# A linear-attention and gated-MLP block on one core: another order of work between the first stage and the z2 stage

## The chip, the cores and the metric

The kernel runs on one core of a Trainium2 chip. The metric is the device time of one execution in microseconds (us). Three executions of the kernel before took 614.0, 615.39 and 615.52 us, with a median of 615.39. Beside them there is one profiled execution, from which all rows of the profile come.

The engines are named as in the profile: PE (TensorE, matmuls; PEld its weight loads), DVE (VectorE), ACT (ScalarE), POOL (GpSimd) and SP (SyncE, which here only issues transfers). Each engine works through its own instructions in a fixed order. A name with a q behind it (SPq, ACTq, POOLq) is the issue of a transfer by that engine.

## The reference

The input x has 2048 rows of 512. It is normalised, and two branches are added to it.

```python
def _A_ref(x, wqkv, w_phi, wo):          # 32 heads of 16
    q, k, v = split(x @ wqkv)
    pq, pk = q @ w_phi, k @ w_phi        # per head
    phi_q = concat(softmax(pq), softmax(-pq))
    phi_k = concat(softmax(pk), softmax(-pk))
    kv, z = phi_k^T v, sum_s phi_k
    return (phi_q kv) / (phi_q z + 1e-6) @ wo

def _B_ref(x, w_in, w_sp, b_sp, w_out):  # F = 1376, halves of 688
    z = gelu(x @ w_in)
    z1, z2 = z[..., :688], layernorm(z[..., 688:])
    g = w_sp @ z2 + b_sp                 # over the rows
    return (z1 * g) @ w_out

xn = layernorm(x)
return x + _A_ref(xn, ...) + _B_ref(xn, ...)
```

All is in float32.

## The kernel before

The rows are worked on in NT = 16 tiles of 128. A float32 operand is held as two parts: `h`, the rounded value (`round_h`, line 61 on ACT), and `l`, the remainder (`rest_l`, line 65, a subtraction, on DVE unless another engine is given). A product is three matmuls, `ah*bh`, `ah*bl` and `al*bh` (`mm3`, lines 69 to 71), so these three lines carry nearly all matmuls.

**First stage** (lines 201 to 501). For each tile: projections for v and for k and q (the small matrix w_phi is first folded into the weights for k and q), and for both of these the two softmaxes (`softmax_pair`, line 120). That takes the maximum and minimum per head (lines 123, 124), two subtractions that write the shifted values (132, 133, "shift"), one exp on ACT (135), sums per head (137) and a reciprocal (138). For k, `normalise` (340) multiplies by the reciprocals on DVE, and a transfer issued by POOL adds the tile to `zacc` (341). `add_kv` (348) adds the tile to the bank `kvps` in matmuls of 32 by 64, with e as one operand and v as the other. For q, the tile of exps is stored to `e_d` (336) for later. Tiles of x are transposed on PE for tiles 0 to 4; for the others a transposed copy of x is loaded (`raw`, 297) and the row means are added to it by a transfer (`nm_d`, 307 and 311). `fetch_T(s)` issues the load of `raw` for a tile and then that of the next plain tile `xt` (208), which has three buffers and is needed for the row statistics (281).

The B branch's input product is split: the first 512 columns of z1 are computed per tile by `z1_raw` (163) with the weight `w1`. This takes 12 matmuls into one of two banks of the PSUM pool `za`, a drain by ACT into the tile `z1f` (168), and a store issued by ACT (169). Of the 16 tiles the loop of the first stage does 11; LAG = 5 are left to the next part.

The weight for everything else, `w2`, has two halves of 432 columns. The raw first half, `w2_raw` (the profile's `w_raw`), has memory of its own and is loaded by eight transfers on SP's queue (`fetch_w2(0, ...)`, lines 174 and 175; written at tile 8 of the loop). The second half is loaded into `staged` tiles (`w2s`) over memory of the first stage.

**The part between** (lines 596 to 668). It splits the two halves of w2 (`split_w2`, `made0` and `made1`), does the last z1 tiles, masks kv (`masked_kv`, 618, into `kvm`, read from `kvps`), sums zacc over the rows on PE (`make_zb`, tile `pz`, and a copy `zb`, 613), transposes kv (`make_kvT`: four transposes 628, a copy on ACT 630, an add on DVE 631), prepares the first operands A of the later stage (`prep_a`: sums S on DVE, 587 to 591, and splits of `wf`, 61 and 65), and weighs two tiles of q's features (`early_features`, 534 to 550, and a transpose 643).

**The z2 stage** (lines 726 to 759). `z2_proj` computes a tile's product with both halves of w2 in 24 matmuls (`zps`). The four pairs of banks are used in turn: the pool of kv, `zc` (which takes the banks of `pz` and `kvt` over), `zb`, `za`. ACT applies gelu, DVE takes statistics, POOL computes the factor (104, 105, 751), and the tiles are normalised and made into operands B.

**Later stages.** The spatial product (`g`, a Strassen-like form with seven products), the gate, the attention output and the last projections.

The order of the instructions on each engine is set by a planner. It goes through the program with a timing model of its own, in which what stands earlier in the program has priority, and what is not ready lets later work pass. `with tc.issue_after(i):` binds what the block issues on the engine of instruction `i` to come behind `i` on that engine; instructions of other engines in the block are not bound. A tile in memory that another pool has used before waits for the tiles that it is laid over.

Of the kernel before, what the change touches and what calls it, by code (L numbers as in the profile page):

```python
# [53 lines left out]
def mixer(ctx: ExitStack, tc: tile.TileContext, x, x_t, wv, wqkT, phi_bd, wo, w_in, wst, b_r, w_out, out):  # L54
# [64 lines left out]

    def softmax_pair(pl, src, tag, scale=1.0, ebufs=2, blocks=1, behind=None):  # L120

        mm = pl.tile([P, 2, H], F32, tag=tag + "mm", bufs=1, name="mm")
        dve.tensor_reduce(mm[:, 0], heads(src), axis=AX.X, op=ALU.max)
        dve.tensor_reduce(mm[:, 1], heads(src), axis=AX.X, op=ALU.min)
        er = pl.tile([P, NF + 2 * H], F32, tag=tag + "e", bufs=ebufs, name="e")
        eb = er.rearrange("p (j c) -> p j c", j=blocks)
        e, r = eb[:, :, :NF // blocks], eb[:, :, NF // blocks:]
        e2 = e.rearrange("p j (h a d) -> p j h a d", a=2, d=DH)
        hd = src.rearrange("p (h j d) -> p j h d", j=blocks, d=DH)
        m = [mm[:, k].rearrange("p (h j) -> p j h", j=blocks).unsqueeze(3).to_broadcast([P, blocks, H // blocks, DH])  # L130
             for k in range(2)]
        dve.tensor_tensor(e2[:, :, :, 0], hd, m[0], op=ALU.subtract)
        softmax_pair.shifted = dve.tensor_tensor(e2[:, :, :, 1], m[1], hd, op=ALU.subtract).ins  # L133
        with tc.issue_after(behind) if behind else ExitStack():
            softmax_pair.exp = act.activation(e, e, AF.Exp, scale=scale).ins  # L135
        sm = pl.tile([P, 2 * H], F32, tag=tag + "sm", bufs=1, name="sm").rearrange("p (j h) -> p j h", j=blocks)
        dve.tensor_reduce(sm, e.rearrange("p j (h d) -> p j h d", d=DH), axis=AX.X, op=ALU.add)  # L137
        dve.reciprocal(r, sm)
        return er
# [12 lines left out]
    def z2_proj(ps, s, w, order):  # L152
# [6 lines left out]
        for k, j in enumerate(order):  # L159
            accumulated(p[k][:, :FW], s, *w[j])  # L160
        return [(slice(k, k + 1), p[k][:, :FW].unsqueeze(1)) for k in range(2)] if ps in (za, kv_ps_p) else [(slice(0, 2), q[:, :, :FW])]
# [15 lines left out]

    def split_w2(dst, raw):
        return [(round_h(act, dst[0][:, c], raw[c]), rest_l(dst[1][:, c], raw[c], dst[0][:, c])) for c in range(ND)]

    LAG = 5
    xT, ahead_of_run = [], []
# [18 lines left out]
    with ExitStack() as p0:  # L201
# [92 lines left out]
        def fetch_T(s):  # L294
            if s < NT:
                raws[s] = wk.tile([P, ND * P], F32, tag="raw", name="raw")
                sp.dma_start(raws[s], x_t[s].rearrange("p a b -> p (a b)"))
                fetch(s + 1)
# [35 lines left out]
        def proj_q(s):  # L334
            e = softmax_pair(wk, proj(s, wqk_h[:, 0], wqk_l[:, 0]), "q", r_x[:, s:s + 1], blocks=NB)
            pool.dma_start(e_d[s], e)

        def normalise(er):
            e = er[:, :NF]
            dve.tensor_tensor(heads(e), heads(e), bc(er[:, NF:], 2 * H), op=ALU.mult)  # L340
            normalise.last = pool.dma_start(zacc, e, accum_op=ALU.add).ins  # L341
# [114 lines left out]
        for s in range(NT):  # L456
# [35 lines left out]
            if s == NT // 2:  # L492
                fetch_w2(0, [w2_raw[:, c] for c in range(ND)])
            if s and s % 2 == 0:
                last = run([t for t in (s + 2,) if t < XT0], feats[:-1])
                behind.close()
                behind.enter_context(tc.issue_after(last))
                del feats[:-1]
        for t, e in feats:
            add_kv(t, e)  # L500
        behind.close()
# [96 lines left out]
    with ExitStack() as p1:  # L598
# [26 lines left out]
        def make_kvT(kvm):  # L625
            pt = psk.tile([P, NG, P], F32, tag="kvt", name="kvt")
            for g in range(NG):
                pe.transpose(pt[:, g], kvm[:, g], ident)
            pt = pt.rearrange("p g (a k b) -> p (g a) k b", k=2, b=QP)
            act.activation(kvT, pt[:, :, 0], AF.Copy)  # L630
            dve.tensor_tensor(kvT, kvT, pt[:, :, 1], op=ALU.add)  # L631

        with ExitStack() as p1a:
# [13 lines left out]
            early = [load_q(s, tb.tile([P, QW], F32, tag="et", bufs=2, name="et")) for s in range(NE)]  # L647
            made0 = split_w2(w2[0], [w2_raw[:, c] for c in range(ND)])[-1]
            for s in range(NT - LAG, NT):
                with tc.issue_after(made0[0]) if s > NT - LAG else ExitStack():  # L650
                    z1_raw(tmp1, s, 2)
                if s == NT - LAG + 1:
                    with tc.issue_after(made0[1]):
                        kvm = masked_kv()
                    with tc.issue_after(z1_raw.last), tc.issue_after(masked_kv.last):
                        made1 = split_w2(w2[1], raw2)[-1]
                if s == NT - 2:
                    make_zb(made1[1])
            with tc.issue_after(z1_raw.pe):
                make_kvT(kvm)  # L660
            raw[0], raw[1] = load_a(0), load_a(1)
            A[0] = prep_a(0, raw.pop(0))
            with tc.issue_after(made1[1]):
                for s in range(NE):
                    early_features(s)
# [61 lines left out]
    for s in range(NT):  # L727
        order = (0, 1) if s % 2 == 0 else (1, 0)
        with tc.issue_after(z1_raw.pe):
            p = z2_proj((kv_ps_p, zc, zbp, za)[s % 4], s, w2, order)  # L730
# [421 lines left out]
```

## Time and profile before

| | us |
|---|---|
| median of three executions | 615.39 |
| profiled execution: time | 615.62 |
| profiled execution: span of the profile | 613.9 |
| first stage: last projection of q issued on PE | 186.94 |
| first matmul of the z2 stage | 205.50 |
| first matmul of the spatial product g | 282.52 |

The span is what the profile covers, from the first to the last instruction or transfer; the 1.7 us beyond it lie around the execution. The granted clock of PE is at 1.00 in the stretches looked at. In the rows of a timeline the first number is the start in us from the span's start, the second the busy time; a bracket gives the idle time of the engine before the instruction and what ended it. Several alike are merged ("x4"). What ended an idle time is inferred from semaphores.

### The profile page before, as it was taken

How to read it: one execution, taken by the hardware profiler on the slowest of the kernel's cores; microseconds unless marked ns; L12 is line 12 of the kernel's file. 1: busy time of each engine (PE TensorE's matmuls, PEld its weight loads, DVE VectorE, ACT ScalarE, POOL GpSimd, SP SyncE). 2: the span in 40 equal slices, each digit the busy share in tenths (PEclk: the TensorE clock that was granted, in tenths of full speed). 3: DMA queues.
4: the chain of work that ended last, by engine and by line, in shares of the span. 5: the costliest groups of instructions: out<-in, count | busy, mean ns of one | idle time of the engine just before them, and what ended most of it. 6: DMA issues, size and time to landing. Idle time of an engine off the chain costs nothing.

```text
span 613.9 us, 11029 instructions
## 1 busy us (share of the span) xinstructions
PE 604.3 (98%) x4059; PEld 537.7 (88%) x4059; DVE 512.7 (84%) x902; ACT 305.3 (50%) x450; POOL 133.2 (22%) x241
## 2 busy tenths in 40 slices
PE   8999999999998999999999999999999999999997
PEld 6778888888887799999999999999999987777786
DVE  5798999999899998678987786878768588999973
ACT  4533333332434457677554545545455755567520
POOL 4243322223111034343000101011010312122200
PEclk9999999999999999999999999999999999999999
DMA  8639776665659720001438767576868989799931
GB/s 322 200 93 199 207 191 151 172 187 126 188 146 242 250 86 22 16 24 48 151 101 214 213 184 232 149 212 190 220 196 219 265 236 251 203 206 244 230 104 69
DMA packets 78322, 106.80 MB, mean 174 GB/s; under 512 B 36956, under 2 KB 46940, under 8 KB 78268
## 3 DMA queue, kind: packets, MB, share of 16 engines
q1 hardware_dynamic: 64268, 61.39, 36.8%
q0 software_dynamic: 11408, 39.98, 24.8%
q10 hardware_dynamic: 2592, 4.72, 2.1%
q8 instruction: 32, 0.52, 0.4%
q14 instruction: 22, 0.18, 0.1%
HBM read 60.30 MB, written 31.09 MB: 149 GB/s over the span
## 4 chain that ended last, share of the span: by engine, by line
PE 89%; DMA 5%; DVE 3%; issue 0%; ACT 0%; SPq 0%; DVEq 0%; ACTq 0%
PE g L70 11%; PE g L71 11%; PE g L69 11%; PE proj L69 6%; PE proj L70 6%; PE proj L71 6%; PE pout L69 6%; PE pout L71 5%; PE pout L70 5%; PE zps L69 4%; PE zps L70 4%; PE zps L71 4%; PE z1ps L69 2%; PE z1ps L70 2%; PE z1ps L71 2%; DMA xt<-in_x 2%
## 5 line engine op out<-in xcount | busy, mean ns | idle before, releaser
L70 PE MATMUL g<-B,A 128*128 128x344 f32 x448 | 143.1, 320 | 0.0
L71 PE MATMUL g<-B,A 128*128 128x344 f32 x448 | 143.1, 319 | 0.0
L69 PE MATMUL g<-B,A 128*128 128x344 f32 x448 | 143.0, 319 | 0.0
L69 PEld LDWEIGHTS g<-B,A 128*128 128x128 f32 x448 | 84.3, 188 | 0.0
L71 PEld LDWEIGHTS g<-B,A 128*128 128x128 f32 x448 | 84.2, 188 | 0.0
L70 PEld LDWEIGHTS g<-B,A 128*128 128x128 f32 x448 | 84.1, 188 | 0.0
L135 ACT ACTIVATE e<-e,r_x 128x1024 f32<-128x1024 f32 x32 | 36.7, 1149 | 62.7 <-DVE e L133 62.7
L61 ACT ACTIVATE A<-S 128x512 fp32r<-128x512 f32 x64 | 39.7, 628 | 52.1 <-PE g L71 24.1
L65 DVE TENSOR_TENSOR A<-S,A 128x512 fp32r<-128x512 f32 x64 | 43.6, 688 | 23.3 <-ACT A L61 22.6
L69 PE MATMUL proj<-wqk_h,xT 128*128 128x512 f32 x124 | 49.2, 396 | 0.0
L61 ACT ACTIVATE A<-wf 128x512 fp32r<-128x512 f32 x64 | 33.2, 521 | 32.1 <-PE g L71 26.3
L71 PE MATMUL proj<-wqk_h,xT 128*128 128x512 f32 x124 | 48.4, 390 | 0.0
L70 PE MATMUL proj<-wqk_l,xT 128*128 128x512 f32 x124 | 48.3, 390 | 0.0
L69 PE MATMUL zps<-w,xT 128*128 128x432 f32 x128 | 46.0, 360 | 1.2 <-DVE kvT L631 1.2
L65 DVE TENSOR_TENSOR A<-wf,A 128x512 fp32r<-128x512 f32 x64 | 35.4, 554 | 13.0 <-ACT A L61 12.6
L70 PE MATMUL zps<-w,xT 128*128 128x432 f32 x128 | 46.1, 360 | 0.0
L71 PE MATMUL zps<-w,xT 128*128 128x432 f32 x128 | 45.8, 358 | 0.0
L137 DVE TENSOR_REDUCE sm<-e 128x64 f32<-128x1024 f32 x32 | 38.5, 1205 | 2.0 <-ACT e L135 1.7
L341 POOL DMA_DIRECT2D zacc<-e x16 | 14.7, 918 | 76.3 <-DVE e L340 22.5
L61 ACT ACTIVATE oT<-po 128x512 fp32r<-128x512 f32 x16 | 8.7, 596 | 41.0 <-PE po L992 41.0
L69 PE MATMUL pout<-wu,uh 128*128 128x512 f32 (+1 forms) x75 | 29.0, 387 | 0.0
L69 PE MATMUL z1ps<-w,xT 128*128 128x512 f32 x64 | 25.4, 396 | 3.0 <-ACT z1f L168 1.6
(182 smaller groups left out, 1427.6 us busy)
## 6 DMA issues: line engine op xcount, KB each, us to landing
wf<-in_wst SPq DMA_DIRECT2D x64, 256.0 KB, 3.8
e_d<-e POOLq DMA_DIRECT2D x16, 544.0 KB, 5.1
et<-e_d SPq DMA_DIRECT2D x64, 136.0 KB, 5.2
zacc<-e POOLq DMA_DIRECT2D x16, 512.0 KB, 4.9
z1t<-z_d POOLq DMA_DIRECT2D x16, 344.0 KB, 6.2
u_d<-c POOLq DMA_DIRECT2D x14, 384.0 KB, 2.8
uT_d<-uT POOLq DMA_DIRECT2D x12, 384.0 KB, 3.2
ut<-uT_d SPq DMA_DIRECT2D x11, 384.0 KB, 7.5
```

The lines of the kernel that those rows point to most:

```text
L61: return act.activation(h, src, AF.Copy).ins
L65: return (eng or dve).tensor_tensor(l, src, h.bitcast(F32), op=ALU.subtract).ins
L69: pe.matmul(dst, ah, bh, start=start, stop=False)
L70: pe.matmul(dst, ah, bl, start=False, stop=False)
L71: return pe.matmul(dst, al, bh, start=False, stop=stop).ins
L135: softmax_pair.exp = act.activation(e, e, AF.Exp, scale=scale).ins
L137: dve.tensor_reduce(sm, e.rearrange("p j (h d) -> p j h d", d=DH), axis=AX.X, op=ALU.add)
L341: normalise.last = pool.dma_start(zacc, e, accum_op=ALU.add).ins
```

## The change

The change moves work around the end of the first stage, in six places:

- The load of w2's first half is bound behind the last transposed x tile that has been issued at that point of the loop (`fetch_T.last`, tile 12), on SP.
- z1 of tiles 11 and 12 is issued on PE behind the last q projection; the exp of that q tile on ACT is bound behind the drain of tile 12, and its two shifts on DVE behind the multiply of the last k tile. z1 of tile 13 follows, with its drain behind that exp. LAST = 2 tiles (14 and 15) are left for the part between, where `z1f` now has three buffers.
- kv of tiles 14 and 15 is bound on PE behind z1 of tile 13, so that both run together.
- In the part between: the roundings of w2's first half come behind the last exp, the masking of kv behind the last remainder of it, z1 of 14 and 15 behind the kv run on PE and their drains behind the roundings on ACT.
- The remainders of w2's second half go from DVE to POOL, behind POOL's issue of the last sum into zacc.
- On ACT, A's roundings come behind the copy of kvT; on DVE, the early features behind the add of kvT; on PE, z2's tiles come one after the other, the first behind the transposes of kv.

```diff
@@ softmax_pair(..., behind=None, shift_behind=None) @@
-        dve.tensor_tensor(e2[:, :, :, 0], hd, m[0], op=ALU.subtract)
-        softmax_pair.shifted = dve.tensor_tensor(e2[:, :, :, 1], m[1], hd, op=ALU.subtract).ins
+        with tc.issue_after(shift_behind) if shift_behind else ExitStack():
+            dve.tensor_tensor(e2[:, :, :, 0], hd, m[0], op=ALU.subtract)
+            softmax_pair.shifted = dve.tensor_tensor(e2[:, :, :, 1], m[1], hd, op=ALU.subtract).ins
@@
-    def split_w2(dst, raw):
-        return [(round_h(act, dst[0][:, c], raw[c]), rest_l(dst[1][:, c], raw[c], dst[0][:, c])) for c in range(ND)]
-
-    LAG = 5
+    def split_w2(dst, raw, eng=None):
+        return [(round_h(act, dst[0][:, c], raw[c]), rest_l(dst[1][:, c], raw[c], dst[0][:, c], eng)) for c in range(ND)]
+
+    LAG, LAST = 5, 2
@@ proj_q @@
-            e = softmax_pair(wk, proj(s, wqk_h[:, 0], wqk_l[:, 0]), "q", r_x[:, s:s + 1], blocks=NB)
+            p, behind = proj(s, wqk_h[:, 0], wqk_l[:, 0]), None
+            if s == NT - 1:
+                for n in range(2):
+                    with tc.issue_after(proj.last):
+                        z1_raw(wk, NT - LAG + n, 2)
+                behind = z1_raw.last
+            e = softmax_pair(wk, p, "q", r_x[:, s:s + 1], blocks=NB, behind=behind,
+                             shift_behind=normalise.dve if behind else None)
@@ the loop over tiles @@
             if s == NT // 2:
-                fetch_w2(0, [w2_raw[:, c] for c in range(ND)])
+                with tc.issue_after(fetch_T.last):
+                    fetch_w2(0, [w2_raw[:, c] for c in range(ND)])
@@ behind the loop @@
+        for n in range(NT - LAG + 2, NT - LAST):
+            with tc.issue_after(softmax_pair.exp):
+                z1_raw(wk, n, 2)
         for t, e in feats:
-            add_kv(t, e)
+            with tc.issue_after(z1_raw.pe):
+                last = add_kv(t, e)
@@ the part between @@
-            made0 = split_w2(w2[0], [w2_raw[:, c] for c in range(ND)])[-1]
-            for s in range(NT - LAG, NT):
-                with tc.issue_after(made0[0]) if s > NT - LAG else ExitStack():
-                    z1_raw(tmp1, s, 2)
-                if s == NT - LAG + 1:
-                    with tc.issue_after(made0[1]):
-                        kvm = masked_kv()
-                    with tc.issue_after(z1_raw.last), tc.issue_after(masked_kv.last):
-                        made1 = split_w2(w2[1], raw2)[-1]
-                if s == NT - 2:
-                    make_zb(made1[1])
+            with tc.issue_after(softmax_pair.exp):
+                made0 = split_w2(w2[0], [w2_raw[:, c] for c in range(ND)])[-1]
+            with tc.issue_after(made0[1]):
+                kvm = masked_kv()
+            for s in range(NT - LAST, NT):
+                with tc.issue_after(made0[0]), tc.issue_after(last):
+                    z1_raw(tmp1, s, 3)
+                if s == NT - LAST:
+                    with tc.issue_after(normalise.last):
+                        made1 = split_w2(w2[1], raw2, pool)[-1]
+                    make_zb(masked_kv.last)
             with tc.issue_after(z1_raw.pe):
                 make_kvT(kvm)
             raw[0], raw[1] = load_a(0), load_a(1)
-            A[0] = prep_a(0, raw.pop(0))
-            with tc.issue_after(made1[1]):
+            with tc.issue_after(make_kvT.act):
+                A[0] = prep_a(0, raw.pop(0))
+            with tc.issue_after(make_kvT.dve):
                 for s in range(NE):
                     early_features(s)
@@ the z2 stage @@
-        with tc.issue_after(z1_raw.pe):
+        with tc.issue_after(z2_proj.pe if s else make_kvT.pe):
             p = z2_proj((kv_ps_p, zc, zbp, za)[s % 4], s, w2, order)
```

The rest of the diff keeps the instructions that are named here (`fetch_T.last`, `normalise.dve`, `z2_proj.pe`, `make_kvT.pe`, `.act`, `.dve`).

More of the change, by code (lines that the diff above doesn't have):

```diff
@@ L118, in bc, with softmax_pair @@
         return ap.unsqueeze(2).to_broadcast([P, n, DH])
-    def softmax_pair(pl, src, tag, scale=1.0, ebufs=2, blocks=1, behind=None):
+    def softmax_pair(pl, src, tag, scale=1.0, ebufs=2, blocks=1, behind=None, shift_behind=None):
         mm = pl.tile([P, 2, H], F32, tag=tag + "mm", bufs=1, name="mm")
@@ L159, in z2_proj @@
         for k, j in enumerate(order):
-            accumulated(p[k][:, :FW], s, *w[j])
+            z2_proj.pe = accumulated(p[k][:, :FW], s, *w[j])
         return [(slice(k, k + 1), p[k][:, :FW].unsqueeze(1)) for k in range(2)] if ps in (za, kv_ps_p) else [(slice(0, 2), q[:, :, :FW])]
@@ L296, in fetch_T @@
                 raws[s] = wk.tile([P, ND * P], F32, tag="raw", name="raw")
-                sp.dma_start(raws[s], x_t[s].rearrange("p a b -> p (a b)"))
+                fetch_T.last = sp.dma_start(raws[s], x_t[s].rearrange("p a b -> p (a b)")).ins
                 fetch(s + 1)
@@ L339, in normalise @@
             e = er[:, :NF]
-            dve.tensor_tensor(heads(e), heads(e), bc(er[:, NF:], 2 * H), op=ALU.mult)
+            normalise.dve = dve.tensor_tensor(heads(e), heads(e), bc(er[:, NF:], 2 * H), op=ALU.mult).ins
             normalise.last = pool.dma_start(zacc, e, accum_op=ALU.add).ins
@@ L627, in make_kvT @@
             for g in range(NG):
-                pe.transpose(pt[:, g], kvm[:, g], ident)
+                make_kvT.pe = pe.transpose(pt[:, g], kvm[:, g], ident).ins
             pt = pt.rearrange("p g (a k b) -> p (g a) k b", k=2, b=QP)
-            act.activation(kvT, pt[:, :, 0], AF.Copy)
-            dve.tensor_tensor(kvT, kvT, pt[:, :, 1], op=ALU.add)
+            make_kvT.act = act.activation(kvT, pt[:, :, 0], AF.Copy).ins
+            make_kvT.dve = dve.tensor_tensor(kvT, kvT, pt[:, :, 1], op=ALU.add).ins
         with ExitStack() as p1a:
```

## The prediction

> **What bounds the kernel now.** First the top of the page: how busy each engine is.
>
> ```profile
> span 613.9 us, 11029 instructions
> PE 604.3 (98%) x4059; PEld 537.7 (88%) x4059; DVE 512.7 (84%) x902; ACT 305.3 (50%) x450; POOL 133.2 (22%) x241
> ```
>
> PE is busy for 604.3 of 613.9 us. The change alters none of its products, so it can only win or lose idle time of PE. Next, then, the view of waits for PE alone, over the whole span (what PE waited for: us in total, times, the longest):
>
> ```profile
> PE z1ps L69 <- ACT z1f L168: 1.6, 1, 1.6
> PE z1ps L69 <- DVE wqk_l L65: 1.4, 1, 1.4
> ...
> PE zps L69 <- DVE kvT L631: 1.2, 1, 1.2
> PE pz L610 <- DMA zacc<-e: 0.3, 1, 0.3
> ```
>
> These four waits are what the change can reach: 4.5 us. The timeline of PE places them (start, us, instruction, idle before it and what ended that):
>
> ```profile
> 11.62 0.63 PE L323 MATMUL pt<-ident,xt 128*128 128x128 f32 x4
> ...
> 34.59 0.39 PE L71 MATMUL proj<-wv_h,xT 128*128 128x512 f32 x1
> 36.38 0.50 PE L69 MATMUL z1ps<-w,xT 128*128 128x512 f32 x1 [1.40 <-DVE wqk_l L65]
> ...
> 177.84 1.10 PE L348 MATMUL kvps<-e,v 128*32 128x64 f32 x64
> ...
> 187.26 0.65 PE L348 MATMUL kvps<-e,v 128*32 128x64 f32 x32
> 187.84 0.50 PE L69 MATMUL z1ps<-w,xT 128*128 128x512 f32 x1
> ...
> 196.22 0.65 PE L348 MATMUL kvps<-e,v 128*32 128x64 f32 x32
> 198.43 0.50 PE L69 MATMUL z1ps<-w,xT 128*128 128x512 f32 x1 [1.55 <-ACT z1f L168]
> ...
> 201.72 0.64 PE L610 MATMUL pz<-zacc,ones 128*32 128x256 f32 x8 [0.26 <-DMA zacc<-e]
> ...
> 210.70 0.36 PE L71 MATMUL zps<-w,xT 128*128 128x432 f32 x1
> 212.24 0.47 PE L69 MATMUL zps<-w,xT 128*128 128x432 f32 x1 [1.19 <-DVE kvT L631]
> ```
>
> One gap lies at 35 us, three between 196 and 212. Matmuls overlap: one is shown with 0.39 us, but the 36 of three z1 tiles went from 187.84 to 196.22, so one starts every 0.23; those of w2, with 432 columns in place of 512, every 0.20 by that. A gap therefore costs the distance of two starts less one step, and after a stop the first matmul is longer by 0.11 (0.50 against 0.39, 0.47 against 0.36).
>
> **The w2 load (start of the kernel).** From the chain of waits, and then the timeline of DVE:
>
> ```profile
> 15.37 6.03 DMA w_raw<-in_w_in
> ...
> 21.50 4.05 DMA xt<-in_x
> ```
>
> ```profile
> 25.57 0.69 DVE L281 BATCH_NORM_STATS2 st<-xt 128x6 f32<-128x512 f32 x1 [2.62 <-DMA xt<-in_x]
> ```
>
> SP issues in order. The eight pieces of w2's first half hold its queue from 15.37 until 21.50, when the next x tile is issued, though the transposes that free its buffer ended at 11.62 + 0.63 = 12.25. It lands 4.05 us after issue, and DVE stands still for 2.62 us. All that DVE does until the wqk_l remainder which frees z1ps's bank is then late by up to that. With the load gone from here the tile is issued some 6.1 us sooner and is there by about 20, before DVE asks at 25.57 - 2.62 = 22.95. The remainder comes up to 2.62 us sooner, more than the 1.40 that PE waits. **Gain: 36.38 - 34.59 - 0.23 = 1.56, and 0.11 of the restart: 1.67.** The lower bound is 0 (another load on the same queue, or the transfers ahead, hold the tile just as long).
>
> Where the load goes instead, behind raw tile 12, SP has this next:
>
> ```profile
> 115.48 0.54 SPq L307 DMA_DIRECT2D nm_d<-nmT  x1
> 124.65 0.33 SPq L297 DMA_DIRECT2D raw<-in_x_t  x1
> ```
>
> Eight issues that took 6.13 us above now stand ahead of a store of row means. Even if it is put off by all of that, to 121.6, the raw tile onto which these means are added is itself issued only at 124.65. So I take 0, up to 1 us if the transfers push the stores of e.
>
> **The z1 tiles and the kv run.** Now PE has q's last projection, then z1 of tiles 11, 12 and 13, kv of tiles 14 and 15 in one run, z1 of 14, pz, z1 of 15, the transposes of kv, then w2's tiles in order. In the kernel before it is ACT's order that makes the gaps:
>
> ```profile
> 194.84 1.15 ACT L135 ACTIVATE e<-e,r_x 128x1024 f32<-128x1024 f32 x1 [3.26 <-DVE e L133]
> 195.90 1.91 ACT L61 ACTIVATE w<-w_raw 128x432 fp32r<-128x432 f32 x4
> 197.71 0.67 ACT L168 ACTIVATE z1f<-z1ps,r_x 128x512 f32<-128x512 f32 x1
> ...
> 205.46 0.42 ACT L61 ACTIVATE A<-wf 128x256 fp32r<-128x256 f32 x1 [4.16 <-DVE S L591]
> 205.54 0.33 ACTq L169 DMA_DIRECT2D z_d<-z1f  x1
> ...
> 209.83 0.69 ACT L168 ACTIVATE z1f<-z1ps,r_x 128x512 f32<-128x512 f32 x1 [2.14 <-DMA z_d<-z1f]
> 210.42 0.38 ACT L630 ACTIVATE kvT<-kvt 128x256 f32<-128x256 f32 x1
> ```
>
> First gap: z1 of tile 12 is drained at 197.71, behind the last exp and four roundings of w2; until then z1 of 14 has no bank. The change puts this drain ahead of the exp: PE ends that tile near 187.3 + 24 x 0.23 = 192.8, the drain takes 0.67, and the exp could not begin before 194.84 anyway, since DVE is late with its input. So the exp's new wait costs nothing, with 1.3 us to spare. **Gain: 198.43 - 196.22 - 0.58 (a run of 32, from 187.26 to 187.84) = 1.63.** Next late is z1 of 15, whose bank waits for tile 13's drain behind the exp: done about 196.7, needed at 199.9.
>
> pz waited for zacc's last sum, issued after the multiply of tile 15. That multiply now stands ahead of the last shift:
>
> ```profile
> 193.52 0.69 DVE L132 TENSOR_TENSOR e<-proj,mm 128x512 f32<-128x512 f32 x1 [1.11 <-DMA e_d<-e]
> ...
> 194.73 1.22 DVE L340 TENSOR_TENSOR e<-e 128x1024 f32<-128x1024 f32 x1
> ...
> 198.24 2.09 DVE L65 TENSOR_TENSOR w<-w_raw,w 128x432 fp32r<-128x432 f32 x4
> ...
> 200.85 0.41 DVE L587 TENSOR_TENSOR S<-wf 128x256 f32<-128x256 f32 x1
> ```
>
> It fills the 1.11 us in which DVE waited for a store, so the shift is put off by 0.1 and the sum leaves 2.3 us sooner. **Gain: 0.26**, the wait shown.
>
> Third gap: at 205.46 ACT had stood for 4.16 us before a piece of A; z1f's store and the next drain stood behind it, that drain waited 2.14 for the store, and kvT's copy came at 210.42, its add after it. Now A is behind kvT's copy, the early features behind its add, and z1f has three buffers. PE transposes kv near 203; copy and add take some 0.4 each, so the banks are free near 204, and they are asked for when w2's first tile is through, 24 x 0.20 = 4.8 later. **Gain: 212.24 - 210.70 - 0.20 + 0.11 = 1.45.**
>
> One kv run in place of two saves 2 x 0.65 - 1.10 = 0.20 and one restart of 0.11: **0.31**. It waits for the multiply of 15 (over near 193.7, needed at 195.5). The masking of kv now stands behind w2's first remainders on DVE. What is ahead of those (store, shift, exp) stays, so they end as now, at 198.24 + 2.09 = 200.3 or sooner, kvm 0.7 later at 201.0; the transposes want it at 202.7. Spare: 1.7.
>
> **The remainders on GpSimd.** No row shows a 128x432 one there. The nearest, and a small instruction of POOL twice:
>
> ```profile
> 28.86 2.53 POOL L65 TENSOR_TENSOR w<-wrow,w 128x512 fp32r<-128x512 f32 x2
> ...
> 224.50 0.27 POOL L751 TENSOR_SCALAR nb<-mv,rstd 128x1 f32<-128x1 f32 x1
> ...
> 225.87 1.67 POOL L751 TENSOR_SCALAR nb<-mv,rstd 128x1 f32<-128x1 f32 x1
> ```
>
> ```profile
> 225.80 0.88 DVE L698 TENSOR_TENSOR T<-z 128x688 f32<-128x688 f32 x1 [0.97 <-ACT z L722]
> 226.61 0.88 DVE L65 TENSOR_TENSOR B<-z,B 128x688 fp32r<-128x688 f32 x1
> ```
>
> 1.27 each at 512 columns gives 1.07 at 432, 4.3 for four; DVE takes 2.09 for as many. DVE is lighter by that, which is worth nothing by itself. But the small instruction took 1.67 in place of 0.27 while DVE ran two subtractions: POOL stood for about as long as they lasted. So the bounds are 4.3 us, and 4.3 plus all that DVE subtracts or multiplies meanwhile. ACT rounds w2's first half until near 198.4 and the second from then on, so POOL starts near 199; DVE's own remainders (to 200.3) and four sums for A (0.41 each) cost it up to 3: the pieces are ready near 202, 203.3, 205 and 206.3. PE wants them at 203.1 + 2.4 + 0.2 = 205.7 and every 0.6 after, to 207.5. It fits by over 1 us; it doesn't if DVE takes A and features sooner. **I take a loss of 0.2, bounds 0 and 2.2.** Behind them POOL has nothing until w2's first statistics.
>
> By the Trainium skill, GPSIMD Engine Reference, section 8 (Key points), GpSimd shares its SBUF interfaces with VectorE and contends with DVE instructions that have two SBUF inputs. That speaks against this edit, and the two rows (0.27 and 1.67) agree.
>
> **The sum.** 1.67 + 1.63 + 0.26 + 1.45 + 0.31 - 0.2 = 5.1 us. The profiled execution has a span of 613.9 and took 615.6, 0.2 above the median of 615.4; 615.4 - 5.1 = 610.3. What comes after must keep pace, or the gain is given back:
>
> ```profile
> 40.00:187.00 147.00, 147.00 (x1062) 120.59 (x1060) 140.48 (x228) 52.27 (x63) 38.75 (x57) 1.00 0.70 175
> ...
> 240.00:282.00 42.00, 42.00 (x216) 40.13 (x215) 30.36 (x58) 31.25 (x55) 16.76 (x26) 1.00 0.08 20
> ```
>
> (Columns: stretch, length, busy PE, PEld, DVE, ACT, POOL, clock, DMA.) While w2's tiles run, DVE needs 30.36 of 42, so a backlog is worked off before the next stage, and PE waits nowhere behind 212.24: the gain is carried to the end.
>
> **Rivals.** (1) *GpSimd late:* POOL stands whenever DVE has two inputs in SBUF, and PE waits 1 to 2.2: 611.2 to 612.4. For it: 1.67; against: over 1 us spare. (2) *The x tile wasn't held by w2:* the gap at 36.38 stays: 612.0. For it: nothing shows when the tile was ready to be issued; against: 25.57 is just 4.05 behind the issue at 21.50, and that just behind w2's last piece. (3) *A new wait for the old:* buffers in the same memory come free later (z1f of tile 13 and its store now use a pool over which A and the sums are laid), kvm or kvT comes 3 us late, and the three gaps from 196 to 212 are given back: about 613.6. (4) *Slower:* one load moves, and the planner's model re-sorts all queues of the first stage. From 40 to 187 DVE is busy 140.48 of 147: 6.5 us in hand. If in the new order 20 of the 32 sums wait one microsecond for their exp, DVE loses 20; PE, with no idle there, gets what passes the 6.5, as it runs out of PSUM banks: 13.5 - 5.1 = 8 slower, 624. It decides from 6.5 + 5.1 = 11.6 on. For it: DVE at 96%; against: over these 147 us PE now waits for nothing.
>
> **How the numbers follow.** The forecast (609.3 to 611.1) 0.55; (1) 0.16; (2) 0.11; (3) 0.10; (4) 0.08. Predicted: 610.3. The range goes from 609.0 to 613.8 and leaves out (4), half of (3) and a little below. About 0.3% (1.8 us) is what a measurement of this kernel can tell from no change: forecast, (1) and (2) are faster, 0.82; (3) is within, 0.10; (4) slower, 0.08.
>
> **What would show it.** No wait of PE near 36 for wqk_l, and the x tile issued near 15.4; the w_raw loads behind 112; one kv run of 64 at the end of the stage; no wait of z1ps for z1f nor of zps for kvT; four POOL rows of w, from 1.07 up; w2's first tile from near 201.5 (203.1 less 1.6). I am wrong if PE waits over 1 us for remainders of POOL, if the first gap stays, or if waits of PE appear between 40 and 187.

## The result and the profile after

| | before | after |
|---|---|---|
| median of four executions on one chip, us | 615.37 | 609.32 |
| lowest to highest, us | 614.0 to 615.52 | 608.96 to 609.71 |
| profiled execution: time, us | 615.62 | 609.71 |
| profiled execution: span, us | 613.9 | 608.0 |

The ratio is 0.9907, with a 95% interval from 0.989 to 0.9924. The kernel is 6.05 us faster; 5.1 was forecast, and 609.32 lies in the range of 609.0 to 613.8. The profiled execution shows 5.9 of it. All medians are over every execution of a version; the ratios leave out two executions at a much lower clock, 661.47 us in experiment 1 and 622.0 in experiment 9. First the top of the page:

```profile
span 608.0 us, 11036 instructions
PE 602.8 (99%) x4059; PEld 537.4 (88%) x4059; DVE 510.3 (84%) x898; ACT 305.5 (50%) x450; POOL 138.9 (23%) x245
```

PE has as many instructions as before. Its idle time, span less busy time, fell from 9.6 us to 5.2, and its busy time, as the profile counts it, by 1.5. The latter fits what was said of the rows: a matmul is shown with 0.39 us though one starts every 0.23, so one ahead of a gap counts more than its step, and there is one run of kv less. The view of waits of PE, over the whole span, has three rows left:

```profile
PE idle L399 <- DVE warm L412: 1.3, 1, 1.3
PE proj L262 <- ACT xT L61: 0.3, 1, 0.3
PE pt L324 <- DVE xt L316: 0.2, 1, 0.2
```

All four waits of 0.3 to 1.6 us that the prediction listed are gone, and no new one is listed. What is left belongs to the start of the kernel. Where the time went is read from marks on PE's timeline, the same product in both kernels (first after, then the one mark of before that has not been shown):

```profile
34.27 0.39 PE L71 MATMUL proj<-wv_h,xT 128*128 128x512 f32 x1
34.49 0.39 PE L69 MATMUL z1ps<-w,xT 128*128 128x512 f32 x1
...
184.94 0.39 PE L71 MATMUL proj<-wqk_h,xT 128*128 128x512 f32 x1
...
193.42 1.10 PE L356 MATMUL kvps<-e,v 128*32 128x64 f32 x64
...
200.11 0.64 PE L623 MATMUL pz<-zacc,ones 128*32 128x256 f32 x8
200.68 0.66 PE L641 MATMUL kvt<-ident,kvm 128*128 128x128 f32 x4
201.09 0.44 PE L69 MATMUL zps<-w,xT 128*128 128x432 f32 x1
...
276.67 0.32 PE L69 MATMUL g<-B,A 128*128 128x344 f32 x1
...
604.26 0.28 PE L71 MATMUL pout<-woh,oT 128*128 128x256 f32 x1
```

```profile
610.14 0.28 PE L71 MATMUL pout<-woh,oT 128*128 128x256 f32 x1
```

| stretch on PE | before | after | gain | forecast |
|---|---|---|---|---|
| start to last projection of q | 186.94 | 184.94 | 2.00 | 1.67 |
| from there to the first zps | 18.56 | 16.15 | 2.41 | 1.63 + 0.26 + 0.31 = 2.20 |
| from there to the first g | 77.02 | 75.58 | 1.44 | 1.45 - 0.2 |
| from there to the last matmul | 327.62 | 327.59 | 0.03 | 0 |
| sum | | | 5.88 | 5.1 |

Every stretch that was to win did, by about its forecast, and nothing was given back behind it.

Timelines of the other engines of the kernel after show how the parts stand to each other. First SP, at the start and at the place to which the load went, then DVE, at the start and between the stages:

```profile
14.87 10.10 SPq L209 DMA_DIRECT2D xt<-in_x  x4
...
110.49 0.42 SPq L175 DMA_DIRECT2D w_raw<-in_w_in  x1
...
115.53 0.54 SPq L308 DMA_DIRECT2D nm_d<-nmT  x1
```

```profile
22.73 0.69 DVE L282 BATCH_NORM_STATS2 st<-xt 128x6 f32<-128x512 f32 x1
...
197.69 0.68 DVE L631 TENSOR_TENSOR kvm<-kvps,mask 128x512 f32<-128x512 f32 x1
...
202.13 1.25 DVE L600 TENSOR_TENSOR S<-wf 128x256 f32<-128x256 f32 x1 [0.89 <-DMA wf<-in_wst]
...
204.42 0.41 DVE L644 TENSOR_TENSOR kvT<-kvT,kvt 128x256 f32<-128x256 f32 x1
```

The x tile is issued at 14.87, not 21.50, and DVE comes to its statistics at 22.73 with no idle time in the bracket, where it stood for 2.62 us before. The load is issued from 110.49 on, just ahead of the store of row means at 115.53. That store was put off: DVE had written its data at 113.45, 2.08 us earlier, where in the kernel before the store went out at 115.48, 0.03 behind its data. Nobody waited for it: POOL issued the transfer that adds these means at 129.70 and at 131.70 before, earlier by just the 2.0 us that the start had won. ACT and POOL between the stages:

```profile
190.81 0.69 ACT L169 ACTIVATE z1f<-z1ps,r_x 128x512 f32<-128x512 f32 x1 [2.03 <-PE z1ps L71]
...
192.77 1.15 ACT L136 ACTIVATE e<-e,r_x 128x1024 f32<-128x1024 f32 x1 [1.28 <-DVE e L134]
...
201.38 0.38 ACT L643 ACTIVATE kvT<-kvt 128x256 f32<-128x256 f32 x1 [0.47 <-PE kvt L641]
...
204.73 0.42 ACT L61 ACTIVATE A<-wf 128x256 fp32r<-128x256 f32 x1 [2.45 <-DMA e_d<-e]
```

```profile
198.72 4.37 POOL L65 TENSOR_TENSOR w<-w2s,w 128x432 fp32r<-128x432 f32 x4 [1.89 <-ACT w L61]
```

The drain of tile 12 ends at 191.50, and the exp behind it still waits 1.28 us, for DVE and not for the drain. A still stands on ACT, for 2.45 us, but now behind kvT's copy, where nobody waits for it. POOL makes the four remainders in 4.37 us; the last is ready at 203.09. A tile's 24 matmuls are 12 with the first half of w2 and 12 with the second, so PE comes to the second half at 203.53 and to the last of the four remainders at 205.48, 2.4 us after it is ready. PE asks for kvT's banks with the second tile, at 205.87; kvT's add on DVE ends at 204.83, 1.0 us ahead.

Set side by side, instruction for instruction, the two kernels have the same order on PE, DVE, ACT and POOL until near the end of the first stage; only SP's differs, by the eight loads that moved. The planner sorted nothing anew there. One place differs from the forecast: pz comes behind z1 of both tiles 14 and 15 and not between them.

### The profile page after: what moved, and what is told of

Read it like the earlier page. It is cut to its first block, busy times and chain, and to the rows that moved or that the text cites. A ratio compares the mean times of both kernels' runs of the same rounds, so it can differ in the third digit from the quotient of the medians.

```text
span 608.0 us, 11036 instructions
## 1 busy us (share of the span) xinstructions
PE 602.8 (99%) x4059; PEld 537.4 (88%) x4059; DVE 510.3 (84%) x898; ACT 305.5 (50%) x450; POOL 138.9 (23%) x245
## 4 chain that ended last, share of the span: by engine, by line
PE 99%; DVE 0%; ACT 0%; issue 0%
PE g L70 12%; PE g L71 12%; PE g L69 12%; PE proj L69 7%; PE proj L71 7%; PE proj L70 7%; PE pout L69 6%; PE pout L71 5%; PE pout L70 5%; PE zps L70 4%; PE zps L69 4%; PE zps L71 4%; PE z1ps L69 2%; PE z1ps L70 2%; PE z1ps L71 2%; PE kvps L356 1%
## 5 line engine op out<-in xcount | busy, mean ns | idle before, releaser
L329 ACT ACTIVATE v<-proj,r_x 128x512 f32<-128x512 f32 x16 | 11.0, 687 | 39.4 <-PE proj L71 36.9
```

The costliest lines, as they stand in the source:

```text
L329: ins = act.activation(v[s], proj(s, wv_h, wv_l, rest_last), AF.Copy, scale=r_x[:, s:s + 1]).ins
```

## The experiments

The theory was the prediction's: the load at the start and the order between the stages are two gains that don't depend on each other, and the second comes from ACT's and DVE's order. The rivals were that one part carries all of it, that the remainders on POOL cost or bring time, and that waits come back as soon as one part is missing. Each experiment changes one thing, of the kernel after or of the kernel before. Times are medians; a ratio is to the kernel before on the same chip. The experiments ran on three chips, where the kernel before has medians from 615.16 to 616.39 us, so a variant's distance from the 609.32 of the kernel after is uncertain by about 1 us. Where that is too coarse, the stretches between marks of PE decide; in the kernel after they are 16.15 us from q's last projection to the first zps and 75.58 from there to the first g.

**1. The load alone, in the kernel before.**

```diff
             if s == NT // 2:
-                fetch_w2(0, [w2_raw[:, c] for c in range(ND)])
+                with tc.issue_after(fetch_T.last):
+                    fetch_w2(0, [w2_raw[:, c] for c in range(ND)])
```

> The kernel before, with the load of w2's first half alone bound behind raw tile 12. In this program only SP's order differs from the kernel before; PE, ACT, DVE and POOL keep theirs. Theory (the load held the x tile, which held DVE, which held PE): the wait of PE for wqk_l is gone, 1.7 to 2.0 us less, 613.5. Rival (the tile is held by something else, or the gain is lost in the last part because DVE and ACT come no sooner there): 615.4, with a longer wait of z1ps for z1f.

613.1 us, ratio 0.9971 (0.9959 to 0.9984): 2.1 less than the 615.17 beside it. The one profiled execution, however, took 615.67. Its timeline of PE, then one stretch of it (length, busy PE, PEld, DVE, ACT, POOL, granted clock, DMA share, GB/s), then its waits of PE:

```profile
195.69 0.50 PE L69 MATMUL z1ps<-w,xT 128*128 128x512 f32 x1 [1.73 <-ACT z1f L168]
...
196.40 0.63 PE L71 MATMUL z1ps<-w,xT 128*128 128x512 f32 x1
```

```profile
195.00:199.40 4.40, 3.71 (x10) 2.89 (x11) 4.38 (x10) 3.54 (x8) 0.69 (x2) 0.62 1.03 276
```

```profile
PE po L993 <- issue: 1.7, 1, 1.7
```

Behind the first gap, which this kernel still has, PE's clock was granted at 0.62 for a few us and a matmul took 0.63 in place of 0.39; and far behind one product waited 1.7 for nothing that the profile shows, and another 0.9 for DVE. So a profiled execution is a witness for waits here and the median for time. By the median the load is worth 2.1 (1.8 by the ratio), about what the start showed. The waits for pz and kvT aren't seen in this execution; PE came to both later, by what the clock cost, so this says nothing about their causes.

**2. The change without the load.**

```diff
             if s == NT // 2:
-                with tc.issue_after(fetch_T.last):
-                    fetch_w2(0, [w2_raw[:, c] for c in range(ND)])
+                fetch_w2(0, [w2_raw[:, c] for c in range(ND)])
```

> The changed kernel with the load of w2's first half back where it was. Only SP's order differs from the changed kernel. Theory: the first part of the gain is lost alone, the rest stays: 2.0 us more than the changed kernel, 611.3, with PE waiting 1.4 for wqk_l near 36 and nowhere else. Rival (the parts lean on each other, the last part needs DVE early): waits of PE near 195 to 206 come back too, 612 or more.

610.88 us, ratio 0.9928 (0.9915 to 0.9942): 1.56 above the kernel after (1.3 by the two ratios). Its waits of PE and its timeline of DVE:

```profile
PE z1ps L69 <- DVE wqk_l L65: 1.4, 1, 1.4
...
PE fold L239 <- DVE wqk_l L65: 0.7, 2, 0.4
```

```profile
25.83 0.70 DVE L282 BATCH_NORM_STATS2 st<-xt 128x6 f32<-128x512 f32 x1 [3.58 <-DMA xt<-in_x]
```

The stall of DVE and the wait near 35 us are back, with a second, smaller one in the folds; the gaps between the stages stay away: the two stretches behind q's last projection are 16.15 and 75.58 us, as in the kernel after. With the first experiment this makes two independent parts: 2.1 for the load alone and 615.17 - 610.88 = 4.3 for the rest alone, together 6.4 where 6.05 were measured, which agrees to within 0.4.

**3. The remainders back on DVE.**

```diff
-                        made1 = split_w2(w2[1], raw2, pool)[-1]
+                        made1 = split_w2(w2[1], raw2)[-1]
```

> The changed kernel with the remainders of w2's second half on DVE again. Theory (the place of these remainders is worth next to nothing, since DVE stands idle for over 3 us between kvm and the sums for A): 0 to 0.4 us more, 609.5. Rival (GpSimd is needed, DVE's 2.1 us come off the path to kvT's add and the features): 1 to 2 us more, with zps waiting for w or kvT from DVE.

609.48 us, ratio 0.9905 (0.9889 to 0.992), and PE has no wait beyond the three of the kernel after. In the time the move to POOL brings and costs nothing. In DVE's timeline the first sum for A has its plain length:

```profile
201.58 0.43 DVE L600 TENSOR_TENSOR S<-wf 128x256 f32<-128x256 f32 x1 [1.04 <-DMA wf<-in_wst]
...
204.67 0.42 DVE L644 TENSOR_TENSOR kvT<-kvT,kvt 128x256 f32<-128x256 f32 x1
```

The four remainders, 2.2 us of work, stand behind that sum and ahead of kvT's add, not in DVE's idle time. The add ends at 205.09; the first zps is at 200.39, so 24 x 0.20 later, at 205.2, PE asks for the banks. The spare of 1.0 us is down to 0.1, and the stretch to the first g is 75.73 us, 0.15 longer. So the move to POOL is worth at most that, and it leaves more spare.

**4. Both halves' remainders on POOL.**

```diff
-                made0 = split_w2(w2[0], [w2_raw[:, c] for c in range(ND)])[-1]
+                made0 = split_w2(w2[0], [w2_raw[:, c] for c in range(ND)], pool)[-1]
```

> The changed kernel with the remainders of both halves of w2 on GpSimd: the suspected cost doubled. Eight of 1.09 from 195.4 on end near 204.2, where the last is wanted at 205.4. Theory (GpSimd keeps its 1.09, and it is DVE's subtractions from two SBUF tiles that are held while GpSimd runs: in the changed kernel the first sum S took 1.25 instead of 0.41): the first S is longer still, about 2.1 us, kvT's add comes near 205.9, PE waits 0 to 0.4: 609.3 to 609.7. Rival (GpSimd is held by DVE, as the prediction had it): the eight take well over 8.7 us and PE waits 1 or more for w, 610.3 or more.

610.79 us, ratio 0.9928 (0.9915 to 0.9942): 1.47 slower than the kernel after (1.3 by the ratios), more than was expected. The loss lies between the first zps and the first g, 77.15 us in place of 75.58. The masking of kv was bound behind a remainder that is no longer on DVE; it now comes earlier, at 194.74, and has no part in the loss. POOL's timeline, DVE's, and PE's waits:

```profile
195.91 4.35 POOL L65 TENSOR_TENSOR w<-w_raw,w 128x432 fp32r<-128x432 f32 x4
200.23 4.39 POOL L65 TENSOR_TENSOR w<-w2s,w 128x432 fp32r<-128x432 f32 x4
```

```profile
200.91 4.00 DVE L600 TENSOR_TENSOR S<-wf 128x256 f32<-128x256 f32 x1 [0.61 <-DMA wf<-in_wst]
```

```profile
PE zps L69 <- DVE kvT L644: 1.1, 1, 1.1
```

POOL was not held: 1.09 us for each of its eight. It was DVE that stood. A sum of two operands in SBUF, 0.43 us by itself (experiment 3), took 4.00, and it ended at 204.91, which is 0.29 behind the end of POOL's run at 204.62. In the kernel after the same instruction took 1.25 and ended at 203.38, again 0.29 behind the end of POOL's run at 203.09. So DVE's sum got through only when POOL was done. kvT's add stands behind the sums, and PE waited 1.1 for it.

Not every run shows a stop to the end of POOL's work. In experiment 7 four remainders took POOL 5.11 us, and three sums of DVE got in between, in DVE's timeline:

```profile
204.91 1.33 DVE L600 TENSOR_TENSOR S<-wf 128x256 f32<-128x256 f32 x1
```

These three took 1.33, 1.36 and 1.23, and each ended 0.28 to 0.29 behind the end of one of POOL's instructions, which lasted 1.29 to 1.32 each. So there both engines paid. What decides whether DVE gets in between isn't shown.

**5. A free on ACT, the early features only behind the masking of kv.**

```diff
-            with tc.issue_after(make_kvT.act):
-                A[0] = prep_a(0, raw.pop(0))
-            with tc.issue_after(make_kvT.dve):
+            A[0] = prep_a(0, raw.pop(0))
+            with tc.issue_after(masked_kv.last):
```

> The changed kernel without the order that puts A's roundings behind kvT's copy on ACT and the early features behind kvT's add on DVE. The planner then puts two pieces of A ahead of kvT's copy. The second of these waited for a store of e until 204.7 in the changed kernel, so the copy comes at about 205.2 and the add, now behind two remainders of A, at about 206.7; PE asks for the banks at 205.8. Theory (A ahead of the copy made the third gap): PE waits about 1 us for kvT, 0.8 to 1.5 us more than the changed kernel, 610.1 to 610.8. Rival (the gap came from the z1 drains and the early w2 alone, and the order of A is of no account): no wait, 609.3.

609.2 us, ratio 0.9887 (0.9851 to 0.9923): no loss, so the expectation failed. The order on ACT that it was to restore did come back, in ACT's timeline:

```profile
203.53 0.42 ACT L61 ACTIVATE A<-wf 128x256 fp32r<-128x256 f32 x1 [2.75 <-DMA z_d<-z1f]
...
203.86 0.36 ACT L643 ACTIVATE kvT<-kvt 128x256 f32<-128x256 f32 x1
```

The copy comes behind a standing piece of A again, some 3 us later than it could. DVE's add behind it and PE's first zps in the same execution:

```profile
204.47 0.41 DVE L644 TENSOR_TENSOR kvT<-kvT,kvt 128x256 f32<-128x256 f32 x1
```

```profile
200.33 0.44 PE L69 MATMUL zps<-w,xT 128*128 128x432 f32 x1
```

The add ends at 204.88, and PE asks for the banks only 24 x 0.20 behind 200.33, near 205.1. On DVE two remainders of A came ahead of the add, and the features stayed behind it. Neither binding is needed in the kernel after; that of A is 0.2 us from being needed.

**6. Two buffers for z1f in place of three.**

```diff
-                    z1_raw(tmp1, s, 3)
+                    z1_raw(tmp1, s, 2)
```

> The changed kernel with two buffers for z1f in the part between instead of three. All engines keep their order. Theory (only two tiles are left there, so a third buffer serves nobody; what counted is that the store of an earlier tile is no longer waited for): no difference, 609.3. Rival (the third buffer, or the shift of the tiles behind it in memory, is part of the gain): a wait for a store or for a transfer returns, 0.5 us or more.

609.01 us, ratio 0.9888 (0.9844 to 0.9933), with the same order on every engine. The third buffer serves nobody.

**7. The two drains behind the exp again.**

```diff
-                for n in range(2):
-                    with tc.issue_after(proj.last):
-                        z1_raw(wk, NT - LAG + n, 2)
                 behind = z1_raw.last
...
-        for n in range(NT - LAG + 2, NT - LAST):
+        for n in range(NT - LAG, NT - LAST):
             with tc.issue_after(softmax_pair.exp):
```

> The changed kernel with z1 of tiles 11 and 12 not bound ahead of the last exp: all three drains stand behind it on ACT. Theory (the drains' place on ACT makes the first gap): z1 of 13 has no bank until the exp is through and tile 11 is drained, about 194.5 where PE could begin at 190.7; PE waits 3.5 to 3.8 us for z1f, and everything behind is that much later: 612.8 to 613.1. Rival (PE has other work, pz or kv, to put there, or later slack takes it up): under 2 us more, below 611.3.

615.67 us, ratio 0.9993 (0.9969 to 1.0018). The whole gain is lost, 6.3 us by the medians and 5.3 by the two ratios (0.9993 - 0.9907, of 615); some 3.6 were expected, so the expectation was too low. PE's timeline and one stretch of it:

```profile
189.80 0.39 PE L71 MATMUL z1ps<-w,xT 128*128 128x512 f32 x1
194.03 0.80 PE L69 MATMUL z1ps<-w,xT 128*128 128x512 f32 x1 [3.84 <-ACT z1f L169]
...
195.05 0.63 PE L71 MATMUL z1ps<-w,xT 128*128 128x512 f32 x1
...
197.14 0.40 PE L70 MATMUL z1ps<-w,xT 128*128 128x512 f32 x1
```

```profile
192.00:196.00 4.00, 1.97 (x5) 1.59 (x6) 2.41 (x4) 2.30 (x3) 1.15 (x3) 0.71 0.80 168
```

PE does two tiles of z1 in this kernel, has no bank for the third and waits 3.84 us. That gap is longer than before's 1.55, since here both drains stand behind the exp. And it costs more than itself: the seven matmuls from 194.03 to 197.14 took 3.11 us in place of 7 x 0.23 = 1.61, at a granted clock of 0.71. So 194.03 - 189.80 - 0.23 = 4.0 for the gap and 1.5 for the clock make 5.5. The Trainium skill, TensorE: Matmul & The Clock Gate, section "HAM oscillation — how this bites in real kernels", says that idle gaps of PE over some 3.4 us throttle its clock. Here 3.84 did; in the first experiment 1.73 did as well, once, and the 1.55 of the kernel before did not in its profiled execution. The mean granted clock of whole executions says how often: it is 0.997 or less in all 12 of this experiment, in 11 of 58 of the kernel before, and in one of the 41 of kernels without the first gap (the kernel after and experiments 2 to 6, 8 and 11); that one is the profiled execution of experiment 8, with another gap of 3.4.

**8. The last shifts not bound behind the multiply.**

```diff
-                             shift_behind=normalise.dve if behind else None)
+                             shift_behind=None)
```

> The changed kernel with the last shift no longer behind the multiply of tile 15 on DVE: the multiply comes after the two shifts again, 1.3 to 2.4 us later. Theory: the kv run, which needs the multiply, is asked for at 193.4 and waits 0.5 to 0.7 for it; zacc's last sum lands by about 199.5 and pz, asked for at 200.1, doesn't wait; 0.5 to 0.8 us more, 609.8 to 610.1. Rival (the place of the multiply is worth only the 0.26 of the wait of pz that the prediction gave it, or nothing): 609.3 to 609.6.

609.74 us, ratio 0.9902 (0.9864 to 0.9939): not to be told from the kernel after, where 0.5 to 0.8 more was expected. The profiled execution took 614.54, and its waits of PE show one far behind the edit:

```profile
PE po L1006 <- issue: 3.4, 1, 3.4
```

From the first g to the last matmul it needed 333.05 us in place of 327.59. Ahead of that PE's stretches are those of the kernel after, 16.15 and 75.58, and PE waited neither for kv nor for pz. In DVE's timeline the wait that the multiply was to fill is short here:

```profile
189.97 0.69 DVE L133 TENSOR_TENSOR e<-proj,mm 128x512 f32<-128x512 f32 x1 [0.17 <-DMA e_d<-e]
```

0.17 us against the 1.11 before: the store came in time. So the order of the two is worth nothing that the trace shows, and the wait of pz is gone without it.

**9. The order of A and the features alone, in the kernel before.**

```diff
-            A[0] = prep_a(0, raw.pop(0))
-            with tc.issue_after(made1[1]):
+            with tc.issue_after(make_kvT.act):
+                A[0] = prep_a(0, raw.pop(0))
+            with tc.issue_after(make_kvT.dve):
```

> The kernel before, with only A's roundings put behind kvT's copy on ACT and the early features behind kvT's add on DVE. Theory (the prediction's third step: the piece of A that stood for 4.16 us with a drain and a store behind it made the third gap; either this order or earlier z1 tiles cures it): the wait of zps for kvT is gone, the other three stay, 1.4 us less than the kernel before. Rival (the gap comes from the late z1 drains, with two z1f buffers, whatever A does): the wait stays within 0.5 of its 1.19.

615.09 us, ratio 0.9992 (0.9973 to 1.0011). In the time there is no gain. In the trace the third gap is gone: from the first zps to the first g (207.12 to 282.70) it is 75.58 us, as after, where before had 77.02, and in DVE's timeline the add comes right behind the copy, with DVE free ahead of it:

```profile
208.69 0.42 DVE L631 TENSOR_TENSOR kvT<-kvT,kvt 128x256 f32<-128x256 f32 x1 [2.46 <-ACT kvT L630]
```

The other waits stay, the first of them at 1.8. So this order removes the wait by itself. Whether the kernel before gains 1.4 us by it isn't settled: the interval reaches to a gain of 1.7 and to a loss of 0.7. In this one execution the 1.44 was lost again ahead of the edit, where q's last projection came at 188.00 in place of 186.94 and the first zps 19.12 behind it in place of 18.56.

**10. Three buffers for z1f alone, in the kernel before.**

```diff
-                    z1_raw(tmp1, s, 2)
+                    z1_raw(tmp1, s, 3)
```

> The kernel before with three z1f buffers in the part between and nothing else; all engines keep their order. The last drain no longer waits 2.14 us for a store and kvT's copy comes some 2 us sooner, at about 208.3; its add stands on DVE behind a feature multiply and a sum, at 211.8, with no idle time in front of it. Theory: the add isn't moved, the wait of zps stays, the time is that of the kernel before. Rival (the store's wait was the cause): the wait is gone, 1.4 us less.

615.56 us, ratio 1.0008 (0.999 to 1.0026): nothing. PE still waits for kvT, 0.7 in place of 1.19, as its first zps came 1.1 later and the add only 0.7. DVE's timeline says why it waits at all:

```profile
209.52 1.22 DVE L534 TENSOR_TENSOR tq<-et,zb 128x1024 f32<-128x1024 f32 x1
...
212.45 0.41 DVE L631 TENSOR_TENSOR kvT<-kvT,kvt 128x256 f32<-128x256 f32 x1
```

The add has no idle time ahead of it: DVE was at a feature's product, its reduction and the sums for A. It is DVE's queue that held PE, not the store of z1f in front of the copy.

**11. Two kv runs again.**

```diff
         for t, e in feats:
-            with tc.issue_after(z1_raw.pe):
+            with tc.issue_after(z1_raw.pe) if t == NT - 1 else ExitStack():
                 last = add_kv(t, e)
```

> The changed kernel with kv of tile 14 no longer bound behind z1 of tile 13: the planner puts most of it right behind the last projection of q, so PE enters the kv bank twice again. Theory: one more run and restart, 0.3 us more, near what can be told, and no wait. Rival: no difference, or a wait as the multiply of tile 14 is late.

610.03 us, ratio 0.9914 (0.9901 to 0.9926): 0.7 above the kernel after, with no wait. PE's timeline:

```profile
184.42 0.39 PE L71 MATMUL proj<-wqk_h,xT 128*128 128x512 f32 x1
...
190.18 0.54 PE L356 MATMUL kvps<-e,v 128*32 128x64 f32 x22
...
193.60 0.86 PE L356 MATMUL kvps<-e,v 128*32 128x64 f32 x42
...
201.08 0.44 PE L69 MATMUL zps<-w,xT 128*128 128x432 f32 x1
```

From q's last projection to the first zps it is 16.66 us in place of 16.15: a second run costs 0.5 here, 0.3 in the runs themselves (0.54 + 0.86 against 1.10) and the rest in the change between the two kinds of product. The start was 0.5 earlier in this execution, which hides that in its span.

## Why the prediction was right, point by point

**What bounds the kernel.** Right. The four waits of PE went, and the time went with them. The 5.9 is more than the 4.5 of the four waits, as the prediction's own sum of distances was: a gap costs more than the wait that is listed for it.

**The load of w2.** The mechanism was right (experiments 1 and 2, from both sides), and the x tile was issued at 14.87 where 15.4 was said. The size was 2.00 in place of 1.67. The gap near 36 gave its 1.56 and 0.11; the other 0.32 had been lost ahead of that gap, since the last projection before it is at 34.27 and no longer at 34.59. Of this, 0.14 belongs to the execution: the transposes that free the buffer are at 11.48 in place of 11.62, before the load can act. From these transposes to q's last projection it is 175.32 us before and 173.46 after, and 173.46 in experiment 1 too, so the load alone is worth 1.86. The 0.18 beyond the prediction lies with the folds: 64 of them, at 29.78 before and 29.64 after, took 1.33 and 1.16 us, and in experiment 2, with the early load, they are listed as waiting for remainders of DVE. The prediction counted the one wait that the profile lists at the top and not the smaller ones of the same cause. That the load costs nothing at its new place was right, and for the reason given: the store behind it was put off by 2.08 us, and the transfer that needs it came late enough.

**The first gap.** Right, and experiment 7 shows that the two drains ahead of the exp are what closes it: with them back behind it, the gap is there again, longer. The exp waited for DVE and not for the drain, as said; the spare was 1.28 where 1.3 had been worked out.

**pz and the one kv run.** pz waits for nothing now, as forecast, but the reason given isn't confirmed. The multiply ahead of the shift was to do it, and without that order pz doesn't wait either (8). PE also does pz later than forecast, behind z1 of 15; which of this and the earlier sum closes the wait was not taken apart. That its 0.26 came out is in part luck. The single run was priced at 0.31 and is worth about 0.5 (experiment 11). The price took the runs' lengths and one restart, and left out what the change of product costs on the way back. That can be the 0.2 by which this stretch gained more than was said; pz's new place, which saves one such change too, can be part of it. kvm was ready at 198.37, 2.3 us ahead of its transposes, where 1.7 was said.

**The third gap.** The size was right, 1.44. Of the reasons given, one fell: the three buffers for z1f do nothing, with the change (6) or alone (10). The binding of A and of the features removes the wait by itself (9), but in the kernel after it isn't what holds the gap closed (5): there the other moves leave ACT and DVE done in time either way. Which of them does it (the earlier z1 tiles, or DVE's remainders on POOL) was not tried one by one. The gap had two remedies and the prediction counted on one.

**The remainders on GpSimd.** This is the step that failed, though it was small. "POOL stood for about as long as they lasted" was taken from two rows of a small instruction, and from it a loss of 0.2. In the kernel after POOL did not stand: 1.09 us each, near the 1.07 that was worked out from widths, and the last was ready 2.4 us early. It is DVE that pays, by 0.84 in the kernel after (1.25 against 0.41) and by 3.6 with twice the work on POOL. There was room for 0.84, so nothing is lost and up to 0.15 is gained (3), and there was none for 3.6 (4). POOL's own price appeared in experiment 7, 1.28 each in place of 1.09, with no wait of PE for it. The Trainium skill, GPSIMD Engine Reference, section 8 (Key points), names the contention, and the runs agree: 1.25 and 4.00 against 0.41 to 0.43 on DVE.

**The rivals.** GpSimd late: not as described; its price, 1.1 of a wait, appeared only when its work was doubled, and by the other engine. The x tile not held by w2: refuted by 14.87 and experiment 1. A new wait for the old: refuted in the time; its mechanism is seen, in A's 2.45 us on ACT for memory that a store of e holds, behind the copy and so without a price. The planner sorts anew: it did not in the first stage.

**The sum.** 5.1 was too low by 0.33 for the start (0.14 of it the execution's), 0.2 for the kv run with the place of pz, and 0.2 for a loss that isn't there: 5.83 of the 5.88 in the profile. The step from 5.88 to the 6.05 of the medians is within the spread of executions.

Not settled: why a late product waited 1.7 us in one execution (1) and 3.4 in another (8) for no visible cause, when a gap of under 2 us takes PE's clock down, what decides between DVE and POOL, and why the order of A alone (9) shows no gain in time. No run gave a version faster than the changed kernel beyond what can be told apart, and the only waits that PE has left lie at the kernel's start.

## What to carry to other kernels

Where one engine is at 98%, list its waits one by one, go back from each to the instruction that stood in the wrong place on another engine's queue, and add up the gaps; the smaller waits of the same cause belong in the sum. A transfer that is needed late but is issued early takes its price from whatever stands behind it on the issuing queue, here an x tile and through it DVE and PE. An instruction moved off a busy engine is worth next to nothing if that engine was not ahead of the bound, and on GpSimd it can hold up the very engine that it was meant to relieve. When an order that was meant to close a gap is in, take it out again: here two gaps stayed closed without the order to which they had been credited.

## What the runs showed of the hardware

- A VectorE sum (S) with two operands in SBUF, 0.41 to 0.43 us by itself, took 1.25 and 4.00 while GpSimd worked through subtractions of 128x432 one behind another, and ended both times 0.29 behind the last of them, GpSimd keeping 1.09 for each. In experiment 7 three such instructions took 1.23 to 1.36, each got through 0.28 to 0.29 behind one subtraction of GpSimd, and these took 1.29 to 1.32.
- A gap of 3.84 us on PE was followed by matmuls of 0.63 in place of 0.39 and a granted clock of 0.71 over four us, 1.5 us on top of the gap. In one execution a gap of 1.73 was followed by the same, at 0.62. The mean clock was 0.997 or less in 12 of 12 executions with the long gap, 11 of 58 of the kernel before, with a gap of 1.55 in its trace, and one of 41 without the gap, and that one had another gap of 3.4.
- A second run of 32-column products between products of the full width cost 0.5 us, of which only 0.3 show as length of the runs.
